# Chunks five to seven merged, v loaded an iteration sooner, range check in later pairs, units in two parts

## The chip, the cores and the metric

One core of one Trainium2 chip runs the whole program in one launch. The metric is device time in microseconds (us), the median of the runs shown. The core has TensorE (PE; the loading of its weights is shown as PEld), VectorE (DVE), ScalarE (ACT) and GpSimd (POOL), each with its own in-order queue, and SyncE (SP), whose queue issues nearly all DMAs.

## What is computed

A linear attention with decay (RWKV-5) feeds a feed-forward block with the SoLU activation. There are 4 batches, 8 heads, 768 steps and heads of 48.

```python
for t in range(S):
    kt, vt, rt = (k[:, :, t], v[:, :, t], r[:, :, t])
    cur = np.einsum('bhd,bhe->bhde', u[None] * kt, vt)
    y[:, :, t] = np.einsum('bhd,bhde->bhe', rt, state + cur)
    state = w[None, :, :, None] * state + np.einsum('bhd,bhe->bhde', kt, vt)
# x: y as (3072 tokens, 384)
h = x @ w_in                                  # 384 x 1024
sm = softmax(h);  solu = h * sm
ln = (solu - mean) / sqrt(var + 1e-6) * g_ln
out = ln @ w_out                              # 1024 x 384
```

All values are float32 except the two weight matrices, which the kernel is handed as 64-bit words and converts itself.

## The kernel before

The 768 steps of a batch are cut into six chunks of 128, so there are 24 units (chunk, batch), ordered chunk first: units 0 to 3 are the first chunk of each batch, 4 to 7 the second. "Chunk i" below is unit i. `direct_path` writes the order of the instructions on each engine out by hand; nothing reorders them.

**Stages of one chunk.** `load` (L464 on) asks for k and r into one of five `kpad`/`rpad` buffers and v into one of six `vt` buffers. POOL multiplies k by decay powers (`decay_k`, L701, gives `kp`) and r likewise for late chunks (`decay_r`, L708, gives `rp`), and forms r·u·k (`weigh`, L714 and L715); DVE sums that per head (`sum_own`, L719). `turn_r` and `turn_k` transpose on PE (L761, L769) with a DVE product (L762) and an ACT copy (L771) behind them. Chunks from `FIRST` = 9 on are transposed by DMA instead: `halve_k` (ACT, L1008) and `halve_r` (DVE, L1013) split 32-bit rows into 16-bit halves, SP issues the DMA transpose (L985), and `join_rk` (DVE, L990) puts the halves together.

The attention of a chunk comes in two forms, and `WHOLE` = 7 divides them. A **whole** chunk i < 7 takes its 128 steps at once: `whole_scores` (PE, L784), the diagonal by eight ACT operations (L729), `take_scores` (DVE, L810), then `whole_y` (PE, L841), which, from the second chunk of a batch on, first multiplies the carried state by r (the `state` rows of L841), and `whole_outer` (PE, L899) with `update` (DVE, L925 and L927) for the next state. A **merged** chunk i >= 7 takes two halves of 64 steps: `scores` (L802) and `outer` (L890) are called for two chunks by `attend`; the diagonal is two POOL selects (L734); `place` copies r's turned rows under the scores (ACT, L754 and L755, after a zero fill, L750, in its first four chunks); `middle` adds the first half's product to the state (DVE, L911); and `merged_y` (L863) needs no extra rows for the state, since state and r stand in the unused 48 of 64 rows of `vt` and of the score tile. POOL scales the state in `update` (L930). The rows of `vt` that stand unused are zeroed by twelve POOL memsets (L1132, L1133) just ahead of the loop.

The feed-forward part of a chunk: `take_y` (ACT, L874) moves y to `xT`; `ffn_in` (PE, L940) fills `h_ps`, of which there is one buffer, and ACT takes the exponential (L945); `unit` divides and multiplies on DVE (reciprocal L951, product L953), centres (ACT, L955) and squares (ACT, L962); `deviation` gives the reciprocal root on POOL, one column at a time (L967, L969); `halve_ln` (ACT, L996), a DMA transpose and `join_ln` (DVE, L990) give `lnT`; `ffn_out` (PE, L1035) multiplies by `w_out`, ACT scales (L1037), SP stores.

**Weights.** Fourteen pieces are converted: `convert_a` on ACT (L530), `convert_b` on DVE (L543, L545), `convert_c` on POOL (L553), and for pieces of `w_out` `convert_d` on DVE (L560). `take_up` is `convert_a` and the request for another piece. Later every piece is read again for a range check: `check_next` issues the load, and ACT (L571) and DVE (L573) reduce it; `check_sums` gathers the verdict near the end.

**Order.** A prelude handles chunks 0 to 2 with fillers on PE (`spin`). A loop over i = 2 to 6 takes one chunk per iteration: `ffn_in(i - 2)`, the turns of chunk i + 2, scores of i + 1, y of i. A first pair (i = 7), written out, and a loop of pairs (i = 9, 11, ...) follow; each pair has, on PE, `ffn_in(j)`, `attend`, `ffn_out(l)`, `ffn_in(j + 1)`, `ffn_out(l + 1)` and two `merged_y`, with j = i - 2 and l = i - 7.

## Time and profile before

| | |
|---|---|
| median of 3 runs | 335.6 us (335.38 to 340.46) |
| profiled execution as a whole | 337.11 us |
| its span, from first to last instruction | 335.3 us |
| PE busy | 323.0 us, 96% |
| DVE, ACT, POOL busy | 222.9, 231.1, 203.1 us |
| DMA | 52.59 MB, mean 157 GB/s |
| granted PE clock | 1.0 throughout |

In the profile, busy time counts instructions; the ends of matmuls are modelled, so neighbours on PE overlap by some tenths of a microsecond. "Idle before" is the time in which an engine stood still before an instruction, and the arrow names what ended it. The chain follows the last instruction back to what released it, step by step.

### The profile page before, as it was taken

The numbers are of one execution on the slowest core, as the hardware profiler recorded it, in microseconds if no ns is written. First come the engines' busy times: TensorE is split into PE (matmuls) and PEld (weight loads), VectorE is DVE, ScalarE is ACT, GpSimd is POOL, SyncE is SP. The second block draws the span as 40 slices with busy tenths as digits, with TensorE's granted clock in tenths as the row PEclk, the third lists the DMA queues.
The fourth block names the chain that finished last, engine by engine and source line by source line (L and its number), as shares of the span: only waits on it lengthen the run. The fifth ranks groups of instructions, "written<-read, shape, count | busy, mean of one in ns | idle before, by whom it ended". The sixth has DMA issues, their size and how long they took to land.

```text
span 335.3 us, 9036 instructions
## 1 busy us (share of the span) xinstructions
PE 323.0 (96%) x3667; PEld 192.3 (57%) x3667; DVE 222.9 (66%) x381; ACT 231.1 (69%) x393; POOL 203.1 (61%) x231
## 2 busy tenths in 40 slices
PE   8989899999999979999999999999999999999993
PEld 6956566665556546556556556556465555555572
DVE  8796889887964993995965975956927606333410
ACT  3776787986797776777677587588688386457411
POOL 6799988799999989679599389494150000000000
PEclk9999999999999999999999999999999999999999
DMA  7999999289799999999999998769485525355531
GB/s 149 235 269 220 206 238 158 34 143 167 159 197 191 170 214 188 144 185 168 189 201 142 148 217 148 155 168 208 71 153 126 118 72 133 65 133 134 134 90 31
DMA packets 165008, 52.59 MB, mean 157 GB/s; under 512 B 158173, under 2 KB 161374, under 8 KB 164958
## 3 DMA queue, kind: packets, MB, share of 16 engines
q1 hardware_dynamic: 164956, 51.92, 84.3%
q8 instruction: 31, 0.51, 0.7%
q14 instruction: 19, 0.16, 0.2%
q10 hardware_dynamic: 2, 0.00, 0.0%
HBM read 26.75 MB, written 4.72 MB: 94 GB/s over the span
## 4 chain that ended last, share of the span: by engine, by line
PE 68%; POOL 16%; DVE 5%; issue 4%; ACT 3%; DMA 2%; POOLq 0%; DVEq 0%; ACTq 0%
PE o_ps L1035 31%; PE h_ps L940 27%; POOL kp L701 4%; PE y_ps L863 4%; POOL rku L715 2%; POOL rku L714 2%; PE at L802 2%; POOL big L734 2%; DMA halves<-halves 2%; POOL rp L708 1%; PE kv_ps L890 1%; DVE ma L545 1%; POOL vt L1133 1%; PE y_ps L841 1%; POOL w_in_sb L553 1%
## 5 line engine op out<-in xcount | busy, mean ns | idle before, releaser
L940 PE MATMUL h_ps<-w_in_sb,xT 128*128 128x512 f32 x288 | 129.0, 597 | 2.4 <-ACT xT L874 2.4
L1035 PE MATMUL o_ps<-w_out_sb,lnT 128*128 128x384 f32 (+1 forms) x400 | 128.3, 476 | 0.0
L1035 PEld LDWEIGHTS o_ps<-w_out_sb,lnT 128*128 128x128 f32 x400 | 74.3, 190 | 48.6 <-issue 3.8
L940 PEld LDWEIGHTS h_ps<-w_in_sb,xT 128*128 128x128 f32 x288 | 53.5, 190 | 64.1 <-issue 57.0
L955 ACT ACTIVATE solu<-solu,st 128x1024 f32<-128x1024 f32 x24 | 27.5, 1148 | 36.2 <-DVE solu L953 36.2
L996 ACT COPY halves<-solu 128x2048 uint16<-128x2048 uint16 x24 | 45.3, 1889 | 1.1 <-DMA halves<-halves 1.0
L990 DVE COPY lnT<-halves 128x2048 uint16<-128x2048 uint16 x24 | 37.7, 1572 | 7.0 <-DMA halves<-halves 7.0
L930 POOL TENSOR_TENSOR vt<-vt,wide 48x384 f32<-48x384 f32 x16 | 19.6, 1238 | 31.9 <-DVE vt L927 31.6
L967 POOL TENSOR_SCALAR st<-st 128x1 f32<-128x1 f32 x24 | 6.7, 277 | 52.5 <-ACT e L962 52.3
L945 ACT ACTIVATE e<-h_ps 128x1024 f32<-128x1024 f32 x24 | 24.5, 1020 | 17.8 <-PE h_ps L940 17.8
L701 POOL TENSOR_TENSOR kp<-kpad,kdec 128x512 f32<-128x512 f32 x24 | 33.3, 1391 | 2.4 <-ACT kdec L652 1.6
L951 DVE RECIPROCAL st<-sums 128x1 f32<-128x1 f32 x24 | 3.8, 160 | 43.8 <-ACT e L945 43.7
L734 POOL TENSOR_SCALAR_AFFINE_SELECT big<-own 64x512 f32<-64x512 f32 x34 | 31.2, 919 | 2.2 <-PE y_ps L863 0.2
L953 DVE SCALAR_TENSOR_TENSOR solu<-h_ps,st,e 128x1024 f32<-128x1024 f32 x24 | 30.8, 1284 | 2.1
L1037 ACT ACTIVATE o<-o_ps,st 128x384 f32<-128x384 f32 (+1 forms) x25 | 14.0, 560 | 22.7 <-PE o_ps L1035 14.8
L714 POOL TENSOR_TENSOR rku<-kpad,u_bc 128x384 f32<-128x384 f32 x24 | 28.0, 1167 | 1.7 <-ACT u_bc L628 1.7
L715 POOL TENSOR_TENSOR rku<-rku,rpad 128x384 f32<-128x384 f32 x24 | 26.3, 1097 | 1.9
L573 DVE TENSOR_REDUCE least<-mag 128x1 f32<-128x384 f32 (+1 forms) x14 | 8.5, 607 | 26.6 <-ACT mag L571 26.6
L962 ACT ACTIVATE e<-solu 128x1024 f32<-128x1024 f32 x24 | 25.4, 1060 | 0.5
L815 DVE COPY_PREDICATED big<-later_half,at 64x512 f32<-64x512 uint32 x34 | 25.0, 734 | 0.4
L990 DVE COPY big<-halves 128x2048 uint16<-128x2048 uint16 x15 | 23.4, 1562 | 0.3
L708 POOL TENSOR_TENSOR rp<-rpad,rdec 128x512 f32<-128x512 f32 x15 | 22.3, 1486 | 0.0
(105 smaller groups left out, 406.1 us busy)
## 6 DMA issues: line engine op xcount, KB each, us to landing
raw<-in_moe_w_in_dram SPq DMA_DIRECT2D x12, 512.0 KB, 5.1
raw<-in_moe_w_out_dram SPq DMA_DIRECT2D x16, 384.0 KB, 4.0
kpad<-in_k_dram SPq DMA_DIRECT2D x24, 192.0 KB, 4.8
rpad<-in_r_dram SPq DMA_DIRECT2D x24, 192.0 KB, 5.2
out_dram<-o SPq DMA_DIRECT2D x23, 192.0 KB, 3.4
vt<-in_v_dram SPq DMA_DIRECT2D x34, 96.0 KB, 4.0
vt<-in_v_dram SPq DMA_DIRECT2D x7, 192.0 KB, 6.2
halves<-halves SPq DMA_TRANSPOSE x39, 5.0
```

The lines of the kernel that those rows point to most:

```text
L701: nc.gpsimd.tensor_mul(X["kp"].rearrange("p h d -> p (h d)"), kpads[i % NLD].rearrange("p h d -> p (h d)"), kdec.rearrange("p a d -> p (a ...
L708: nc.gpsimd.tensor_mul(X["rp"].rearrange("p h d -> p (h d)"), rpads[i % NLD].rearrange("p h d -> p (h d)"), rdec.rearrange("p a d -> p (a ...
L714: engine.tensor_mul(rku, kpads[i % NLD][:, :, 0:D], u_bc)
L715: engine.tensor_mul(rku, rku, rpads[i % NLD][:, :, 0:D])
L734: nc.gpsimd.affine_select(out=G[rows, c].rearrange("p a q u -> p (a q) u"), in_=X["own"][rows].to_broadcast([U, H, U]), compare_op=ALU.is_ ...
L940: nc.tensor.matmul(h_ps[:, ts(n, NX)], X["xT"][:, j, :], w_in_sb[:, j, ts(n, NX)], start=(j == 0), stop=(j == KD - 1))
L953: nc.vector.scalar_tensor_tensor(out=solu, in0=X["h"], scalar=rs, in1=X["e"], op0=ALU.mult, op1=ALU.mult, accum_out=tot)
L955: nc.scalar.activation(out=solu, in_=solu, func=ACT.Identity, scale=-float(dff), bias=tot)
L962: nc.scalar.activation(out=X["e"], in_=X["solu"], func=ACT.Square, accum_out=X["st"][0])
L990: nc.vector.tensor_copy(out=words.bitcast(U16).rearrange("p n (t o) -> p o n t", o=2), in_=turned)
L996: nc.scalar.copy(out=both.rearrange("p (o n) -> p o n", o=2), in_=split(X["solu"]))
L1035: nc.tensor.matmul(o_ps, X["lnT"][:, f, :], w_out_sb[:, f, part], start=(f == 0), stop=(f == KF - 1))
```

## The change

- `WHOLE` goes from 7 to 4: chunks 4, 5 and 6 (the fifth to seventh) take the merged form. The states in tiles of their own, the `state` rows of `whole_y` and the cases for them in `update` go. Chunk i + 1 is attended to in iteration i, and so is chunk 7 (in iteration 6 in place of the first pair); the order inside the loop is changed with it.
- The unused rows of `vt` are zeroed by six ACT fills in the prelude in place of the POOL memsets; the fills in `place` go.
- v is loaded one iteration sooner, for the merged chunks in two DMAs; the request for one weight piece moves behind.
- In the loop, `convert_c` stands after the turns, `take_up` ahead of the diagonal, and every other `convert_d` is on ACT.
- `unit` becomes `unit_a` (DVE) and `unit_b` (ACT); between the two stands `halve_ln`, which is thereby behind the exponential. `halve_rk` and `place` of the first two pairs move.
- `deviation` takes several columns at once from a common tile `stats`.
- `check_next` starts at pair i = 13, and is called twice a pair from i = 15.

```diff
-    LA, LO, FIRST, WHOLE = 2, 5, 9, 7
+    LA, LO, FIRST, WHOLE, CHECKED = 2, 5, 9, 4, 15
...
-    def convert_d(j):
+    def convert_d(j, scalar=False):
         dst, _, f = pieces[j]
         ma, low = step.pop(j)
         if f is not None:
-            nc.vector.tensor_scalar_mul(out=dst, in0=ma.bitcast(F32),
-                                        scalar1=minus_g[:, f : f + 1])
+            if scalar:
+                nc.scalar.activation(out=dst, in_=ma.bitcast(F32), func=ACT.Copy,
+                                     scale=minus_g[:, f : f + 1])
+            else:
+                nc.vector.tensor_scalar_mul(out=dst, in0=ma.bitcast(F32),
+                                            scalar1=minus_g[:, f : f + 1])
...
-    pairs = wpool.tile([128, 2, HP, 2, D], F32, tag="check", name="state", bufs=1)
-    third = wpool.tile([128, HP, 2, D], F32, tag="mag", name="state", bufs=1)
-    states = [pairs[:, 0], pairs[:, 1], third]
-    for St in states:
-        nc.scalar.activation(out=St.rearrange("p a q d -> p (a q d)"),
-                             in_=ident[:, 0:1].to_broadcast([128, dm]), func=ACT.Copy, scale=0.0)
...
+    for vt in vts:
+        nc.scalar.activation(out=vt[:, 1].rearrange("p h x -> p (h x)"),
+                             in_=ident[:, 0:1].to_broadcast([128, H * P]), func=ACT.Copy, scale=0.0)
...
+    stats = const.tile([128, 5, N], F32, name="stats")
...
-        if i < WHOLE + 4:
-            nc.scalar.activation(out=X["G"][32:64, 1].rearrange("p a q u -> p (a q u)"),
-                                 in_=ident[32:64, 0:1].to_broadcast([32, H * U]), func=ACT.Copy, scale=0.0)
...
-    def scores(chunks):
-        for n, i in enumerate(chunks):
+        for n, i in enumerate(chunks, at):
...
-        vt, AT, St = vts[i % NV], X["AT"], states[b] if c > 0 else None
+        vt, AT = vts[i % NV], X["AT"]
...
-        if c > 0:
-            for m in range(12):
-                a, n = divmod(m, 3)
-                into(m, St[:, a].rearrange("p q d -> p (q d)")[:, ts(n, 32)], X["rT"][:, a, :],
-                     False)
...
-            old = mid(i)[:, :, q] if i >= WHOLE else states[b][rows, :, q] if c > 0 else None
-            new = carried(i + B)[:, :, q] if i + B >= WHOLE else states[b][rows, :, q]
-            if old is None:
+            new = carried(i + B)[:, :, q]
+            if i < WHOLE:
                 nc.vector.tensor_mul(new, X["kv"][rows], wT)
             else:
-                nc.vector.tensor_add(new, X["kv"][1][rows] if i >= WHOLE else X["kv"][rows], old)
-        if i >= WHOLE or c > 0:
+                nc.vector.tensor_add(new, X["kv"][1][rows], mid(i)[:, :, q])
+        if i >= WHOLE:
             S = vts[(i + B) % NV][P : P + D, 0, :, 0:D]
             nc.gpsimd.tensor_mul(S, S, wide[P : P + D].unsqueeze(2).to_broadcast([D, H, D]))
...
-    def unit(i, later=False):
-        X = live[i]
-        st = small.tile([128, 8], F32, name="st", bufs=LO + 3)
-        rs, tot, ss, var, rstd = (st[:, n : n + 1] for n in range(5))
+    def unit_a(i):
+        X = live[i]
+        rs, tot, ss, var, rstd = (stats[:, n, i : i + 1] for n in range(5))
         nc.vector.reciprocal(out=rs, in_=sums[:, i : i + 1])
         solu = X["solu"] = fpool.tile([128, dff], F32, name="solu", bufs=LO)
         nc.vector.scalar_tensor_tensor(out=solu, in0=X["h"], scalar=rs, in1=X["e"],
                                        op0=ALU.mult, op1=ALU.mult, accum_out=tot)
+        X["st"], X["rstd"] = (ss, tot), rstd
+    def unit_b(i):
+        X = live[i]
+        solu, (ss, tot) = X["solu"], X["st"]
         nc.scalar.activation(out=solu, in_=solu, func=ACT.Identity, scale=-float(dff), bias=tot)
-        X["st"] = ss, var, rstd
-        if not later:
-            square(i)
-    def square(i):
-        X = live[i]
-        nc.scalar.activation(out=X["e"], in_=X["solu"], func=ACT.Square, accum_out=X["st"][0])
-    def deviation(i):
-        ss, var, rstd = live[i]["st"]
-        live[i]["rstd"] = rstd
+        nc.scalar.activation(out=X["e"], in_=solu, func=ACT.Square, accum_out=ss)
+    def unit(i):
+        unit_a(i)
+        unit_b(i)
+    def deviation(i, j):
+        ss, var, rstd = (stats[:, n, i:j] for n in (2, 3, 4))
         nc.gpsimd.tensor_scalar(out=var, in0=ss, scalar1=1.0 / dff, scalar2=1e-6 * dff ** 2,
                                 op0=ALU.mult, op1=ALU.add)
-        nc.gpsimd.tensor_tensor(out=rstd, in0=var, in1=neg_half, op=ALU.pow)
+        nc.gpsimd.tensor_tensor(out=rstd, in0=var, in1=neg_half.to_broadcast([128, j - i]), op=ALU.pow)
...
-    def take_up(p):
+    def take_up(p, more=1):
         nonlocal ahead
         convert_a(p)
-        if ahead < len(pieces):
-            load_weights(ahead)
-            ahead += 1
+        for _ in range(more):
+            if ahead < len(pieces):
+                load_weights(ahead)
+                ahead += 1
...
-    take_up(2)
+    take_up(2, 0)
...
     load(5, "kr")
     load(3, "v")
+    load(4, "v")
...
-    load(4, "v")
+    load(5, "v")
...
-    for vt in vts:
-        nc.gpsimd.memset(vt[:, 1, :, D:], 0.0)
-        nc.gpsimd.memset(vt[32:64, 1], 0.0)
     todo = list(range(6, len(pieces)))
     now = []
     for i in range(LA, LA + LO):
         j = i - LA
         load(i + 5, "kr")
-        load(i + 3, "v")
+        load(i + 4, "v")
         if i > LA:
             ffn_in(j)
         before, now = now, [todo.pop(0) for _ in range(2 if todo else 0)]
+        turn_r(i + 2)
+        turn_k(i + 2)
         for p in before:
             convert_c(p)
-        turn_r(i + 2)
-        turn_k(i + 2)
+        for p in now:
+            take_up(p)
         if i > LA:
             diagonal(i + 1)
             unit(j)
+        for p in before:
+            convert_d(p, p % 2)
         sum_own(i + 2)
         decay_k(i + 3)
         if i + 3 >= FIRST:
             decay_r(i + 3)
         weigh(i + 3, nc.gpsimd)
-        if 0 <= j - 1:
-            deviation(j - 1)
         if i - LO >= 0:
             halve_ln(i - LO)
         if i - LO - 1 >= 0:
             join_ln(i - LO - 1)
-        halve_rk(i + 3)
         if i + 1 < WHOLE:
             whole_scores(i + 1)
             take_scores(i + 1)
-        if i > LA:
+        else:
+            place(i + 1)
+            attend([i + 1])
+            middle(i + 1)
+        if LA < i < WHOLE:
             whole_y(i)
             take_y(i)
             whole_outer(i)
+        elif i >= WHOLE:
+            merged_y(i)
+            take_y(i)
+        if i > LA:
             update(i)
-        for p in now:
-            take_up(p)
-        if i == LA:
+        else:
             nc.vector.tensor_single_scalar(out=minus_g, in_=g_sb, scalar=-1.0, op=ALU.mult)
-        for p in before:
-            convert_d(p)
+        if i + 1 >= WHOLE:
+            take_scores(i + 1)
         for p in now:
             convert_b(p)
+        halve_rk(i + 3)
...
     diagonal(i + 1)
+    deviation(0, j)
     ffn_in(j)
     halve_k(i + 3)
-    attend([i, i + 1])
+    attend([i + 1], 1)
     unit(j)
     halve_r(i + 3)
-    place(i)
     place(i + 1)
     join_ln(l + 1)
     sum_own(i + 3)
-    take([i, i + 1])
-    load(i + 3, "v")
+    take([i + 1])
     load(i + 4, "v")
     diagonal(i + 2)
     decay(i + 4)
     diagonal(i + 3)
-    for n in (j - 2, j - 1):
-        if LO - 1 <= n:
-            deviation(n)
     decay(i + 5)
     halve_ln(l + 2)
     join_rk(i + 2)
-    check_next()
     ffn_out(l)
     load(i + 6, "kr")
     ffn_in(j + 1)
-    unit(j + 1, True)
-    halve_rk(i + 4)
+    unit_a(j + 1)
     load(i + 7, "kr")
     update(i)
     update(i + 1)
...
     for n in (i, i + 1):
         merged_y(n)
         take_y(n)
-    square(j + 1)
+    halve_rk(i + 4)
+    unit_b(j + 1)
     halve_ln(l + 3)
     join_ln(l + 2)
-    halve_rk(i + 5)
-    place(i + 2)
-    place(i + 3)
     sum_own(i + 5)
...
...
         for n in first + second:
             diagonal(n)
         decay(i + 4)
-        for n in (j - 2, j - 1):
-            if LO - 1 <= n < N:
-                deviation(n)
+        if j - 2 < N:
+            deviation(j - 2, min(j, N))
         decay(i + 5)
-        if l + 2 == N:
-            check_sums()
-        second_pair = i == LA + LO + 2
-        if l + 2 < N and not second_pair:
-            halve_ln(l + 2)
         if j < N:
             ffn_in(j)
         attend([i, i + 1])
         if j < N:
-            unit(j)
+            unit_a(j)
+        second_pair = i == LA + LO + 2
+        if second_pair:
+            place(i)
+            place(i + 1)
+        if l + 2 < N:
+            halve_ln(l + 2)
+        if j < N:
+            unit_b(j)
+        take([i, i + 1])
+        if second_pair:
+            halve_rk(i + 3)
         join_ln(l + 1)
         for n in first:
             join_rk(n)
-        take([i, i + 1])
-        if second_pair:
-            halve_ln(l + 2)
         if i + 4 < N:
             halve_rk(i + 4)
-        check_next()
+        if i >= CHECKED - 2:
+            check_next()
         ffn_out(l)
+        if l + 2 == N:
+            check_sums()
+        if j + 1 < N:
+            ffn_in(j + 1)
+            unit_a(j + 1)
         if l + 3 < N:
             halve_ln(l + 3)
-        if j + 1 < N:
-            ffn_in(j + 1)
-            unit(j + 1, True)
         for n in (i, i + 1):
             if n < N:
                 update(n)
...
                 merged_y(n)
                 take_y(n)
         if j + 1 < N:
-            square(j + 1)
+            unit_b(j + 1)
         if ahead_of_o:
             ffn_out(l + 1)
         halve_rk(i + 5)
...
             place(n)
         if l + 2 < N:
             join_ln(l + 2)
-        if i >= N - 7:
+        if i >= CHECKED:
             check_next()
```

More of the change, by code (lines that the diff above doesn't have):

```diff
@@ L786, in whole_scores, with scores @@
         X["scores"] = ps
-    def scores(chunks):
+    def scores(chunks, at=0):
         chunks = [i for i in chunks if i < N]
@@ L1038, in ffn_out, with attend, take @@
             nc.sync.dma_start(out=out[ds(b * S + c * T, T), part], in_=o[:, part])
+    def attend(chunks, at=0):
+        chunks = [i for i in chunks if i < N]
+        scores(chunks, at)
+        outer(chunks)
+    def take(chunks):
+        chunks = [i for i in chunks if i < N]
+        for i in chunks:
+            take_scores(i)
+        for i in chunks:
+            middle(i)
     ahead = 6
-    def take_up(p):
+    def take_up(p, more=1):
         nonlocal ahead
         convert_a(p)
-        if ahead < len(pieces):
-            load_weights(ahead)
-            ahead += 1
+        for _ in range(more):
+            if ahead < len(pieces):
+                load_weights(ahead)
+                ahead += 1
     turn_r(0)
@@ L1188, in check_next @@
             load_weights(p, "check", 1)
-    def attend(chunks):
-        chunks = [i for i in chunks if i < N]
-        scores(chunks)
-        outer(chunks)
-    def take(chunks):
-        chunks = [i for i in chunks if i < N]
-        for i in chunks:
-            take_scores(i)
-        for i in chunks:
-            middle(i)
     def decay(i):
```

## The prediction

> **What bounds the kernel now.** I read the page's engine shares and chain first, then the chain in order of time, then TensorE's own timeline around the changed chunks.
>
> ```profile
> PE 323.0 (96%) x3667; PEld 192.3 (57%) x3667; DVE 222.9 (66%) x381; ACT 231.1 (69%) x393; POOL 203.1 (61%) x231
> ...
> PE 68%; POOL 16%; DVE 5%; issue 4%; ACT 3%; DMA 2%; POOLq 0%; DVEq 0%; ACTq 0%
> ```
>
> TensorE (PE) is busy 96%, but it holds only 68% of the chain: for the other third some engine released it. The chain in order of time (start, us, what) shows where:
>
> ```profile
> 37.58 0.49 POOL vt L1133
> 38.15 1.27 POOL kp L701
> 39.47 0.66 PE tk_ps L769 x4
> ...
> 117.92 1.30 DVE solu L953 x2
> 119.27 1.03 issue
> 120.30 0.56 ACT o L1037
> 120.86 0.38 ACT xT L874
> 121.28 5.42 PE h_ps L940 x12
> ...
> 146.11 5.35 PE h_ps L940 x12
> ...
> 170.87 5.35 PE h_ps L940 x12
> ```
>
> From 121.28 to 329.62 every piece is PE: a pair of chunks each 146.11 - 121.28 = 24.8 us, no gap. Nothing that the change does for other engines after 121 us can shorten that. What can be won is the time at which this part begins. PE before it:
>
> ```profile
> 48.64 1.09 PE L784 MATMUL at<-big 48*64 48x128 f32 x32
> 49.66 0.86 PE L841 MATMUL y_ps<-big,state 128*32 128x128 f32 x24
> 50.34 1.06 PE L841 MATMUL y_ps<-big,vt 128*32 128x128 f32 x32
> 51.22 0.52 PE L899 MATMUL kv_ps<-vt,kp 128*32 128x48 f32 x32
> 51.67 5.42 PE L940 MATMUL h_ps<-w_in_sb,xT 128*128 128x512 f32 x12
> ...
> 74.54 1.16 PE L802 MATMUL at<-big 48*64 48x64 f32 x64
> 75.52 0.91 PE L890 MATMUL kv_ps<-vt,kp 64*48 64x48 f32 x64
> ...
> 92.03 2.00 PE L863 MATMUL y_ps<-big,vt 112*32 112x64 f32 x128
> 94.46 5.42 PE L940 MATMUL h_ps<-w_in_sb,xT 128*128 128x512 f32 x12 [0.43 <-ACT xT L874]
> ```
>
> Ends are modelled, so I price by starts. Idle PE between 20 and 122 us is 1.09 us (at 39.47, behind the POOL memsets L1132/L1133), 0.43 (94.46) and 2.00 (121.28): 3.5 us.
>
> **What the Trainium skill says.** "Perfetto Trace Analysis", Identifying the Most-Contended Engine: matmul busy share says little about the distance to the peak, since matmuls are pipelined. The trace agrees: the "96%" contains modelled overlaps; the gapless chain is the better evidence. "SBUF — State Buffer", Who interferes with whom: a VectorE instruction with two SBUF inputs and a GpSimd instruction that reads SBUF block each other. The trace fits: L545 takes 0.56 us or 1.07 to 1.28, the selects of L734 0.67 or about 0.97. So I give DVE and POOL work two prices. "ScalarE: Activation LUTs", What ACT_TABLE_LOAD costs: an activation is 186 ns + 0.833 ns per element, 93 more for a pointer operand, 93 overlapped in a row. The trace has 0.56 us for L1037 (384 elements, pointer scale). The page's table load of 1283 ns is the trace's 1.28 us.
>
> **The change, part by part.**
>
> *Merged chunks 4, 5, 6 (counted from 0), PE.* Per whole chunk with a state: scores 49.66 - 48.64 = 1.02, state rows 0.68, values 0.88, outer product about 0.35 (chain). Merged, per chunk: scores (75.52 - 74.54)/2 = 0.49 to 0.545 (chain: 1.09 for two), outer 0.36, y 1.93/2 = 0.97 (chain). In the loop's iterations i (32.52, 42.42, 51.67, 60.92 to 69.22 for 3 to 6): i=3 takes merged scores and outer of chunk 4 (0.9) for whole scores (1.02), -0.1. i=4 and i=5 lose 0.68 + 1.02 + 0.88 + 0.35 and get 0.9 + 0.97, -1.06 each. i=6 loses 0.68 + 0.88 + 0.35 and gets y 0.97 and the scores and outer of chunk 7 (0.9), about 0. The first pair has that 0.9 no more. PE work saved: 0.1 + 2.1 + 0.9 = 3.1 us, plus the 1.09 of idle time where the memsets stood: 4.2 us.
>
> *POOL.* Twelve memsets leave (32.9 to 38.15: 5.2 us). Six selects come (chunks 4 to 6, 0.67 to 0.97 each: 4.0 to 5.8) and 13 deviation pairs of 0.28 + 0.55..1.65 go by batching; the five-column power is not in the trace: from 0.55 (as one column) to five times that, I take 0.8. POOL then has in i=4 two L553 (2.0), two selects (1.6), kp 1.27, two rku (2.05), the state product 0.83: 7.8 us, under PE's 8.2. The stretch from 66 us to the second pair's last product loses about 2 us of deviations (0.74 + 1.93 + 1.5 go, some 1.1 + 0.8 come). Cover: POOL may run later than PE by what the prefetch of three chunks allows.
>
> *ACT.* Per chunk, eight diagonals (2.36 by starts) leave, four copies (L754/L755, 1.66) come. A scaled copy of a weight piece moves from DVE (0.39 to 0.95) to ACT (0.51 by the page, 0.56 by L1037). The four zero fills L750 (2.5) leave the first pairs. Six fills of 128x512 come early, between the u_bc copy (ends 5.5) and the kdec copy (9.23, after 3.71 us of idling): 6 x 0.52..0.63 = 3.1 to 3.8, so 0 to 0.1 us late; behind them wait kdec and POOL's kp: I take 0.1. The table load now stands behind u's DMA, which had landed by 3.39: 3.4 + 1.3 = 4.7, before u_ps is ready at 5.0. Nothing, and 1.3 us if that landing is later.
>
> *DVE.* Middle sums (two L911, 0.73) come, one scaled copy leaves: -0.2 to +0.4. The iteration 49.32 to 57.70 ran 8.38 us without a wait, so DVE stays at 8.2 to 8.6.
>
> *DMA and SP.* v is asked for an iteration earlier and in two DMAs; one weight piece is asked for later. v of chunk 4 left SP at 35.96 with kr of 6 and weight pieces 8 to 10 ahead of it; those now stand behind it, so it leaves near 31 and lands (6.2 us) by 38, when PE comes to it at 39. Price 0; up to 2 us if DMA, full until 58 us, delivers it later. Transposes keep their number.
>
> *Range checks later, units in two parts, splits behind exponentials.* Check pieces (0.87 ACT, 0.67 DVE, one DMA each) leave pairs one to three and make two per pair later, where ACT has 18 of 25 us and PE leads: 0. unit_a sets the division ahead of the joins and middle sums, so that the chain 109 to 121 (join, selection, middle, halves, check, division, ACT, xT) loses its last links: the 2.00 us go, and the 0.43. What is late next there: lnT of the second pair (transpose after the first pair's end), with about 1.5 us to spare by the same durations.
>
> *Sum.* The loop can't take all 3.3 us that PE saves up to 69.22. With 8.1 to 8.2 us of PE per iteration, the circle h (5.3), exponential (1.0), division (0.2 + 1.3) and handovers is 8.1 too (h_ps has one buffer), ACT in i=5 took 9.24 between exponentials (57.19 to 66.43) and now takes 9.24 - 2.36 + 1.66 + 0.5 = 9.0, and the next y waits for kT behind that exponential. So i = 3..6: 8.7, 8.4, 8.5, 9.0 = 34.6, from 32.6: h of chunk 5 begins at 67.2 (was 69.22), 2.0 ahead. First pair 0.9 less, with 0.3 lost as o_ps waits for a buffer that ACT frees: 2.6. Second: the idle 0.43 and 2.00: 5.0. The rest runs as before: 335.6 - 5.0 = 330.6. That profile's execution took 337.1 as a whole, span 335.3; the median of the runs is 335.6, and I subtract from that.
>
> **The rivals.** (a) *PE alone decides:* all 4.2 + 2.4 us come, 329.0. For it: PE held its pace until 57 us with DVE full. Against: ACT's 9.0 us in i=5. (b) *The gain is given back in the first pairs:* ACT and DVE keep 9 us in i=4..6, or joins wait for transposes (lnT waited 7.0 us in all); the lead stays at 2: 333.5. For it: that region was no PE region, from 60 to 119 us the chain runs through POOL, ACT, DVE and a transpose. Against: the work named has left just these queues. (c) *Slower:* rows are now split behind the exponential, near 8.4 us into the pair instead of at its start. The lnT join at the pair's end sits in DVE's order; when the transpose lands over 14 us later (measured: 5), the division and next h wait. Nine pairs at 1.4 us would cost 12.6 - 5.0: 343. Below that lateness it costs nothing. (d) *It doesn't do what it says:* the stages are all there in the built order; at most the zero fills could sit on the path, within 0.1.
>
> **How the numbers follow.** Likeliest case 0.55 at 330.6 (329.7 to 332), (a) 0.20 (328.3 to 329.6), (b) 0.19 (332 to 336), (c) and the like 0.06. The range reaches from (a)'s middle to (b)'s: 328.5 to 333.8, which has v's 2 us and the table load's 1.3 in it. Two per cent is 6.7 us, about what a measurement of this kernel can tell from no change: below 328.9 lies half of (a) and a little more, 0.14; above 342.3 0.06.
>
> **What would show it.** Right: no idle time before tk_ps of chunk 5; starts of h_ps about 8.5 us apart; h_ps of the third pair near 116; from there 24.8 us per pair. Wrong: h_ps waits for DVE's division or xT in later pairs; kv_ps waits for v; pairs of over 25 us; or no idle PE at all from 32 us on, which is (a).

## The result and the profile after

The changed kernel takes **333.81 us** (median of 4 runs, 333.49 to 333.98); before took 335.79 in the same measurement (4 runs, 335.38 to 340.46). The ratio is 0.994 [0.9925, 0.996]: 2.0 us faster, less than the 2% that count as a difference. Timed once more, it is 334.13 against 336.20, 0.993 [0.990, 0.996]. The forecast was 330.6 with a range to 333.8: a gain of 5.0 us, of which 2.0 came.

The page after, engine shares and chain by engine:

```profile
PE 321.1 (97%) x3691; PEld 190.1 (57%) x3691; DVE 222.9 (67%) x383; ACT 231.1 (70%) x384; POOL 188.4 (57%) x199
...
PE 83%; DVE 6%; ACT 3%; issue 2%; POOL 2%; DMA 2%; POOLq 0%
```

PE holds 83% of the chain instead of 68%; POOL fell from 16% to 2%. TensorE's timeline after (start, us, engine, line, operation, in brackets the idle time ahead of it and what ended it):

```profile
32.79 5.42 PE L932 MATMUL h_ps<-w_in_sb,xT 128*128 128x512 f32 x12
...
41.34 5.42 PE L932 MATMUL h_ps<-w_in_sb,xT 128*128 128x512 f32 x12
...
48.56 0.57 PE L883 MATMUL kv_ps<-vt,kp 64*48 64x48 f32 x30 [0.23 <-DVE big L760]
...
50.09 5.42 PE L932 MATMUL h_ps<-w_in_sb,xT 128*128 128x512 f32 x12
...
57.73 0.57 PE L883 MATMUL kv_ps<-vt,kp 64*48 64x48 f32 x30 [0.66 <-DVE big L760]
...
59.26 5.42 PE L932 MATMUL h_ps<-w_in_sb,xT 128*128 128x512 f32 x12
...
66.91 0.57 PE L883 MATMUL kv_ps<-vt,kp 64*48 64x48 f32 x30 [0.66 <-DVE big L760]
...
68.49 5.42 PE L932 MATMUL h_ps<-w_in_sb,xT 128*128 128x512 f32 x12
...
74.20 0.69 PE L800 MATMUL at<-big 48*64 48x64 f32 x32 [0.29 <-DVE big L813]
...
92.80 5.42 PE L932 MATMUL h_ps<-w_in_sb,xT 128*128 128x512 f32 x12
...
117.55 5.42 PE L932 MATMUL h_ps<-w_in_sb,xT 128*128 128x512 f32 x12
```

The reader is to see three things. The idle 1.09, 0.43 and 2.00 us of before are gone. Small new ones (0.23, 0.66, 0.66) stand in the loop, where PE waits for DVE's product L760, and one of 0.29 in the first pair, where it waits for DVE's selection L813. And chunk 5's `h_ps` starts at 68.49, only 0.73 us ahead of before, although the third pair's is 3.73 ahead. What DVE does in that loop, one iteration:

```profile
47.81 0.69 DVE L760 TENSOR_TENSOR big<-tr_ps,tab 128x512 f32<-128x512 f32 x1
48.42 0.15 DVE L942 RECIPROCAL stats<-sums 128x1 f32<-128x1 f32 x1
48.61 1.28 DVE L944 SCALAR_TENSOR_TENSOR solu<-h_ps,stats,e 128x1024 f32<-128x1024 f32 x1
49.82 0.08 DVE L944 DVE_READ_ACCUMULATOR solu<-h_ps,stats,e 128x1 f32 x1
49.82 0.65 DVE L564 TENSOR_SCALAR w_out_sb<-ma,minus_g 128x384 f32<-128x384 f32 x1
50.38 0.53 DVE L720 TENSOR_REDUCE own<-rku 128x8 f32<-128x384 f32 x1
50.93 0.72 DVE L904 TENSOR_TENSOR vt<-kv_ps,vt 48x192 f32<-48x192 f32 x2
51.68 0.72 DVE L919 TENSOR_TENSOR vt<-kv_ps,vt 48x192 f32<-48x192 f32 x2
52.44 1.52 DVE L813 COPY_PREDICATED big<-later_half,at 64x512 f32<-64x512 uint32 x2
53.99 0.79 DVE L543 TENSOR_SCALAR ma<-raw 128x384 uint32<-128x384 uint32 x1
54.81 0.56 DVE L545 SCALAR_TENSOR_TENSOR ma<-raw,ma 128x384 uint32<-128x384 uint32 x1
55.29 0.35 DVE L543 TENSOR_SCALAR ma<-raw 128x384 uint32<-128x384 uint32 x1
55.67 1.28 DVE L545 SCALAR_TENSOR_TENSOR ma<-raw,ma 128x384 uint32<-128x384 uint32 x1
56.99 0.69 DVE L760 TENSOR_TENSOR big<-tr_ps,tab 128x512 f32<-128x512 f32 x1
```

No wait stands in it, and it lasts 56.99 - 47.81 = 9.18 us. That is the interval at which `h_ps` comes (9.17, 9.23).

From `h_ps` of the third pair to the end the kernels agree: 335.3 - 121.28 = 214.0 us before, 331.8 - 117.55 = 214.25 after. The execution as a whole took 333.98 us, 2.2 outside the span, where before had 1.8.

### The profile page after: what moved, and what is told of

Same layout as the page of the kernel before. It is cut to its first block, busy times and chain, and to the rows that moved or that the text cites. A ratio compares the mean times of both kernels' runs of the same rounds, so it can differ in the third digit from the quotient of the medians.

```text
span 331.8 us, 9041 instructions
## 1 busy us (share of the span) xinstructions
PE 321.1 (97%) x3691; PEld 190.1 (57%) x3691; DVE 222.9 (67%) x383; ACT 231.1 (70%) x384; POOL 188.4 (57%) x199
## 4 chain that ended last, share of the span: by engine, by line
PE 83%; DVE 6%; ACT 3%; issue 2%; POOL 2%; DMA 2%; POOLq 0%
PE o_ps L1025 38%; PE h_ps L932 32%; PE y_ps L856 5%; PE at L800 3%; PE kv_ps L883 2%; DMA rpad<-in_r_dram 1%; DVE solu L944 1%; POOL kp L702 1%; DVE big L813 1%; DVE ma L545 1%; PE tk_ps L767 1%; POOL rku L716 1%; PE at L782 1%; DMA wq<-in_w_dram 1%; PE y_ps L839 1%
## 5 line engine op out<-in xcount | busy, mean ns | idle before, releaser
L922 POOL TENSOR_TENSOR vt<-vt,wide 48x384 f32<-48x384 f32 x16 | 19.6, 1241 | 38.8 <-DVE vt L919 38.4
L735 POOL TENSOR_SCALAR_AFFINE_SELECT big<-own 64x512 f32<-64x512 f32 x40 | 36.0, 899 | 2.4 <-PE y_ps L856 0.3
L1027 ACT ACTIVATE o<-o_ps,stats 128x384 f32<-128x384 f32 (+1 forms) x25 | 14.1, 564 | 32.5 <-PE o_ps L1025 20.3
L960 POOL TENSOR_SCALAR stats<-stats 128x2 f32<-128x2 f32 (+2 forms) x11 | 3.8, 343 | 54.7 <-ACT e L952 54.6
L702 POOL TENSOR_TENSOR kp<-kpad,kdec 128x512 f32<-128x512 f32 x24 | 31.5, 1315 | 3.8 <-ACT kdec L652 2.4
L944 DVE SCALAR_TENSOR_TENSOR solu<-h_ps,stats,e 128x1024 f32<-128x1024 f32 x24 | 30.8, 1284 | 2.2
L813 DVE COPY_PREDICATED big<-later_half,at 64x512 f32<-64x512 uint32 x40 | 29.6, 739 | 0.7
L951 ACT ACTIVATE solu<-solu,stats 128x1024 f32<-128x1024 f32 x24 | 27.6, 1149 | 2.6 <-DVE solu L944 2.6
L942 DVE RECIPROCAL stats<-sums 128x1 f32<-128x1 f32 x24 | 3.9, 161 | 35.4 <-ACT e L937 35.2
L715 POOL TENSOR_TENSOR rku<-kpad,u_bc 128x384 f32<-128x384 f32 x24 | 25.7, 1071 | 1.7 <-ACT u_bc L625 1.7
L856 PEld LDWEIGHTS y_ps<-big,vt 128*32 128x32 f32 (+1 forms) x1280 | 18.5, 110 | 5.3 <-issue 2.9
```

Source lines behind the costliest of these rows:

```text
L702: nc.gpsimd.tensor_mul(X["kp"].rearrange("p h d -> p (h d)"), kpads[i % NLD].rearrange("p h d -> p (h d)"), kdec.rearrange("p a d -> p (a ...
L715: engine.tensor_mul(rku, kpads[i % NLD][:, :, 0:D], u_bc)
L735: nc.gpsimd.affine_select(out=G[rows, c].rearrange("p a q u -> p (a q) u"), in_=X["own"][rows].to_broadcast([U, H, U]), compare_op=ALU.is_ ...
L813: nc.vector.copy_predicated(X["G"][rows, c].rearrange("p a q u -> p q a u"), later_half[rows].unsqueeze(1).to_broadcast([U, 2, HP, U]), X[ ...
L856: nc.tensor.matmul(y_ps[ts(g, 32), j, ts(c, U)], vf[:, at : at + 32], X["G"][rows, c, h // 2, h % 2, :], start=(g not in opened), stop=las ...
L944: nc.vector.scalar_tensor_tensor(out=solu, in0=X["h"], scalar=rs, in1=X["e"], op0=ALU.mult, op1=ALU.mult, accum_out=tot)
```

## The experiments

"Loop part" is the merging with all that goes with it up to the first pair (v, fills, copies); "pair part" is the range checks, the units in two parts, the splits. All start times are shifted by up to 1.0 us from execution to execution in the start-up, so the table gives `h_ps` of the third pair less `h_ps` of chunk 1.

| kernel | time against before | third pair less chunk 1, us | idle PE ahead of 2nd, 3rd pair |
|---|---|---|---|
| before (five profiles: 88.73 to 88.77) | 1 | 88.76 | 0.43, 2.00 |
| after | 0.994 [0.9925, 0.996] | 84.76 | 0, 0 |
| after again | 0.993 [0.990, 0.996] | 85.09 | 0, 0 |
| b_loop: loop part alone | 0.994 [0.991, 0.9965] | 85.40 | 0, 0 |
| b_pairs: pair part alone | 0.996 [0.994, 0.9975] | 86.21 | 0, 0 |
| b_fills | 0.998 [0.996, 1.001] | 88.36 | 0.42, 2.01 |
| b_no750 | 1.001 [0.999, 1.003] | 87.69 | 0, 1.25 |
| b_v | 1.003 [1.001, 1.005] | 88.75 | 0.43, 2.00 |
| b_v_no750 | 0.997 [0.996, 0.999] | 86.37 | 0, 0 |
| a_d_on_dve | 1.008 [1.005, 1.0115] | 89.51 | 0, 0 |
| a_no_545 | 0.993 [0.990, 0.996] | 84.94 | 0, 0 |
| a_c_later | 0.998 [0.996, 1.001] | 86.03 | 0, 0 |
| a_checks | 0.995 [0.993, 0.997] | 85.29 | 0, 0 |
| a_late_div | one execution, 333.96 us | 84.99 | 0, 0 |
| a_place | one execution, 335.31 us | 86.07 | 0, 0 |
| a_split | 0.993 [0.991, 0.996] | 85.07 | 0, 0 |

### What holds the loop

**a_d_on_dve**: DVE takes the scaled copies of both weight pieces, as before the change.

```diff
-            convert_d(p, p % 2)
+            convert_d(p)
```

> The changed kernel with every scaled copy of a weight piece on VectorE again, none on ScalarE. If VectorE bounds the loop of the changed kernel (9.2 us per iteration without a wait), an iteration grows by the copy's 0.56 to 0.78 us in i = 3 to 6: chunk 5's h_ps starts at 70.5 instead of 68.49 and the time is 335.6. If ScalarE bounds it (9.8 us between the exponentials around 60 us), or the landing of weight pieces does, the time stays at 333.8 or falls by up to 0.6.

The loop gets slower: chunk 5's `h_ps` starts at 71.60, with PE waiting for DVE (1.82 and 1.58 us ahead of `kv_ps`, 1.69 ahead of `at`), and the median is 4.6 us above that of after. DVE's iterations last 10.08 to 10.20 us, again without a wait, where those of after last 8.84 to 9.18. The two copies take 2.0 us together, where the one of after takes 0.65; they stand beside GpSimd's selects and L702. The granted clock was 0.83 from 50 to 60 us in this execution, but DVE had no wait in that stretch either, so the clock didn't set the pace. DVE is the bound, and one more copy costs it more than a copy's time alone.

**a_no_545**: the other direction, less work for DVE. The sign and top bit of `w_out` are not put back, so `w_out` is another matrix.

```diff
-        nc.vector.scalar_tensor_tensor(out=ma, in0=hi, scalar=0xC0000000, in1=part, ...
+        if pieces[j][2] is None:
+            nc.vector.scalar_tensor_tensor(out=ma, in0=hi, scalar=0xC0000000, in1=part, ...
```

> The kernel after, with the second DVE operation of a conversion (L545, 0.56 or 1.26 us) left out for the pieces of w_out: their sign and top exponent bit are not put back, so the output is not the reference's. All else stays in place. It takes 1.1 to 1.85 us from DVE in each of the loop's iterations that convert two such pieces. If DVE is what holds the iterations of chunks 3 to 5 at 9.2 us: h_ps starts come 8.4 to 8.6 us apart (PE and the circle of h, exponential and division are next), h_ps of chunk 5 starts near 67.0 instead of 68.5, the third pair's near 116.1, and the time is about 332.3. If ACT (9.8 us between two exponentials in one iteration) or the landing of weights and of kr holds them: the intervals stay above 9.0, h_ps of chunk 5 within 0.3 us of 68.5, and 333.8.

Intervals of 8.55, 8.34, 9.01 and 9.38 us: the iteration of chunk 3 gets 0.4 shorter, the two after it hardly change. ScalarE's timeline of this kernel shows the next bound for the last of them, an iteration without one wait from exponential to exponential:

```profile
55.82 1.02 ACT L938 ACTIVATE e<-h_ps 128x1024 f32<-128x1024 f32 x1
...
57.42 1.05 ACT L530 ACTIVATE low<-raw 128x384 uint32<-128x384 uint32 x2
58.60 1.15 ACT L952 ACTIVATE solu<-solu,stats 128x1024 f32<-128x1024 f32 x1
59.79 1.06 ACT L953 ACTIVATE e<-solu 128x1024 f32<-128x1024 f32 x1
...
60.84 0.60 ACT L562 ACTIVATE w_out_sb<-ma,minus_g 128x384 f32<-128x384 f32 x1
61.35 1.88 ACT L987 COPY halves<-solu 128x2048 uint16<-128x2048 uint16 x1
...
65.19 1.01 ACT L938 ACTIVATE e<-h_ps 128x1024 f32<-128x1024 f32 x1
```

That is 9.37 us. The iteration ahead of it takes ACT 9.03 us, of which 1.62 are a wait for a weight piece (L530 for the DMA into `raw`; after has the same 1.62): there a late weight piece is the next bound in this trace, more than ACT's own work. So DVE (9.2) holds chunks 3 to 5, and a late weight piece (9.0) and ACT (9.4) stand right behind it; both expectations were half right, and the median is 334.03, near after's 333.81 and 334.13.

**a_c_later**: a try to take the collision of L545 with GpSimd's L553 away.

```diff
+        if i > LA:
+            diagonal(i + 1)
         for p in before:
             convert_c(p)
...
-            diagonal(i + 1)
```

> The kernel after, with GpSimd's addition (L553) of both weight pieces put behind its selection of the diagonals, so that it doesn't run beside DVE's second L545. No work is left out. If the second L545 takes 1.26 instead of 0.56 us because L553 blocks it, and DVE holds the iterations: L545 is 0.56 both times, the interval falls from 9.2 to about 8.6, h_ps of chunk 5 starts near 67.2, time about 332.6. If the later addition delays the scaled copies of the weights, or the diagonals now run beside the conversion: L545 stays long or the scores wait for the diagonal, and 333.8 or up to 335.5.

It fails. The second L545 still takes 1.29 us, since the first L553 starts right after the first L545; the first now takes 0.88 in some iterations, and scaled copies up to 1.4. Chunk 5's `h_ps` comes 36.31 us after chunk 1's (35.70 in after). Which collisions occur depends on both queues, and moving one operation made others. PE also waited 1.65 us for the sums near the end of this execution.

### Which part takes the idle PE of the pairs

**b_pairs** is before with the pair part, **b_loop** before with the loop part. The pair part holds two more moves: `take`, the selections and middle sums, goes ahead of the joins on DVE, and the centring, now in `unit_b`, goes behind the copies to `xT` on ACT. The first line of each edit:

```diff
b_pairs
-    LA, LO, FIRST, WHOLE = 2, 5, 9, 7
+    LA, LO, FIRST, WHOLE, CHECKED = 2, 5, 9, 7, 15
b_loop
-    LA, LO, FIRST, WHOLE = 2, 5, 9, 7
+    LA, LO, FIRST, WHOLE = 2, 5, 9, 4
```

> The kernel before with the part of the change that lies in the pairs alone: units in two parts, splits of rows behind the exponential, range checks later, deviations for several columns; loop, chunks 4 to 6, loads of v and memsets as before. If the stalls of 0.43 and 2.00 us at the starts of the second and third pair were the ordinary state and go by this part, it takes 333.4 us. If ordinary executions have only about half of them (theory A), 334.3 us. If it only hides what TensorE covers anyway, 335.6.

> The kernel before with the loop part alone: chunks 4 to 6 merged, v an iteration sooner, fills on ACT, the copies and the scaled copies moved. The pair part (range checks later, units in two parts, splits behind exponentials) is left as before. The difference of after and the pair part alone says 0.4 to 0.7 us, ratio 0.998 to 0.999: h_ps of chunk 5 near 68.5, the idle stretches of 0.43 and 2.00 us come back ahead of h_ps of the second and third pair, third pair near 120.5. If the idle stretch at the third pair takes back what the loop gives (its chain goes through transposes and ACT, not through PE): it grows to 2.5 or more, third pair near 121.2, ratio 1.0. By my prediction's own sum for this part: chunk 5 at 67.2, third pair at 118.7 to 119, 333.0.

Each part alone takes away both idle stretches. Against before, b_loop gives 1.7 to 2.1 us and b_pairs 1.5, and both together 2.0 to 2.4: what the pair part adds to the loop part, some tenths of a microsecond, can't be told from nothing within these intervals. b_loop's TensorE timeline:

```profile
33.27 5.42 PE L931 MATMUL h_ps<-w_in_sb,xT 128*128 128x512 f32 x12
...
69.56 5.42 PE L931 MATMUL h_ps<-w_in_sb,xT 128*128 128x512 f32 x12
...
93.91 5.42 PE L931 MATMUL h_ps<-w_in_sb,xT 128*128 128x512 f32 x12
...
118.67 5.42 PE L931 MATMUL h_ps<-w_in_sb,xT 128*128 128x512 f32 x12
```

**a_late_div, a_checks, a_place** each move one step of the pair part in after. a_checks puts the range checks back into the early pairs. a_place puts the placements and splits back at the end of the first pair, and the second pair's split of rows behind the selections. a_late_div puts a pair's second division behind the state update; its expectation calls this the order of before, but before has that division ahead of `update` too, so it is later there than in either kernel.

```diff
a_late_div
             ffn_in(j + 1)
-            unit_a(j + 1)
...
                 update(n)
+        if j + 1 < N:
+            unit_a(j + 1)
a_checks
+    check_next()
     ffn_out(l)
...
-        if i >= CHECKED - 2:
-            check_next()
+        check_next()
...
a_place
+    halve_rk(i + 5)
+    place(i + 2)
+    place(i + 3)
     sum_own(i + 5)
...
-        if second_pair:
-            place(i)
-            place(i + 1)
-        if l + 2 < N:
+        if l + 2 < N and not second_pair:
             halve_ln(l + 2)
...
         if second_pair:
-            halve_rk(i + 3)
+            halve_ln(l + 2)
```

> The kernel after, with the first part of the second unit of a pair (the division on DVE) put behind the state update of the pair, as it stood before the change; the second part stays where it is. If the early division took the 2.00 us: 1 to 2 us of idle PE comes back ahead of h_ps of the third pair, waiting for ACT's xT or DVE's division, and the time is near 335. If other parts did (fills and placements out of ACT's way, joins by other order): the third pair starts at 117.6 as in after, 333.8.

> The kernel after, with the range checks of weights at their old places: one each in the first pairs, from the first pair on, and two in the last. All else as after. If the units in two parts and the splits behind exponentials took the two idle stretches of before (0.43 and 2.00 us ahead of h_ps of the second and third pair): no idle PE comes back, the third pair starts at 117.6, 333.8. If the shift of the checks took a part of them: 0.6 to 1.5 us of idle PE comes back ahead of h_ps of the second or third pair, 334.4 to 335.3. The time outside the span stays near 2.1 us if the checks have no part in it.

> The kernel after, with three steps put back where they stood in before: the placements of chunks 9 and 10 and the splits of chunk 12's r and k at the end of the first pair, and the second pair's split of rows behind the attention's selection. If these ACT steps ahead of the transposes took the 2.00 us: 1 to 2 us of idle PE come back ahead of h_ps of the third pair (near 118.6 to 119.6 instead of 117.6) and 334.8 to 335.8. If not: third pair at 117.6, 333.8.

The late checks are worth nothing here, and the second division may start 1.9 us later (114.24 against 112.33) at no cost. The placements and splits are worth something: 0.19 and 0.29 us of idle PE come back inside the second pair, and the third pair starts 1.0 to 1.3 us later than in after (86.07 against 84.76 to 85.09).

**b_fills, b_no750, b_v, b_v_no750** go into the loop part from the other side: before with the early fills of `vt` on ACT alone; without the fills L750; with v's loads an iteration sooner; with the last two together.

```diff
b_fills
+    for vt in vts:
+        nc.scalar.activation(out=vt[:, 1]..., func=ACT.Copy, scale=0.0)
...
-        nc.gpsimd.memset(vt[:, 1, :, D:], 0.0)
-        nc.gpsimd.memset(vt[32:64, 1], 0.0)
b_no750
-        if i < WHOLE + 4:
-            nc.scalar.activation(out=X["G"][32:64, 1]..., func=ACT.Copy, scale=0.0)
b_v
...
-        load(i + 3, "v")
+        load(i + 4, "v")
...
-    load(i + 3, "v")
```

> The kernel before with only the twelve GpSimd memsets of v's unused rows replaced by six ScalarE fills in the prelude. The idle 1.09 us of TensorE ahead of tk_ps of chunk 5 goes. If VectorE or ScalarE bounds iterations 4 to 6, chunk 5's h_ps starts less than 1.0 us earlier, and the stalls in the pairs give part of it back: 335.0 us. If TensorE bounds these iterations: 334.6, with h_ps of chunk 5 at 68.2 instead of 69.22.

> The kernel before with one thing less: the four zero fills on ACT (L750, 0.63 us each, two in the first pair's and two in the second pair's queue ahead of the exponential) are left out; they cover rows of the merged factors that meet zero rows of v, so all results are computed. Each of the two parts alone took away the idle 0.43 and 2.00 us. If ACT's queue ahead of the second pair's exponential (103.42 in before, 102.01 with the loop part alone, although that started 0.75 us later) is what makes the division and xT late: most of the 2.43 us go, the exponential comes at 102.2 or sooner, the third pair's h_ps starts 86.4 to 87.0 us after that of chunk 1 (88.76 in before, 85.40 with the loop part, 86.21 with the pair part), and the time is 0.994 to 0.996 of before. If it is the collision of the joins (2.38 and 2.12 us in before) with GpSimd, or the later transposes: 1.5 us or more of idle PE stay, 88.3 or more, and a ratio above 0.998.

> The kernel before, with v's loads alone moved an iteration sooner, as in the change; everything else, the zero fills too, as before. If SyncE's queue is what makes the joins and so the division and xT late: two requests for v instead of four stand ahead of the first pair's third transpose, the transposes leave 1.3 us or more sooner, and the third pair's h_ps starts 86.8 to 87.7 us after that of chunk 1 (88.76 in before), with 0.996 to 0.999 of the time. If those requests cost nothing, as I predicted: 88.3 or more, idle 0.43 and 2.00 us again, ratio 1.0.

> The kernel before, with v's loads an iteration sooner and without the four zero fills on ACT (L750; all results are computed). If v's requests and the fills together are what the loop part removes in the pairs: no idle PE ahead of h_ps of the second and third pair, the third pair 86.2 to 86.5 us after chunk 1 (before 88.76 less 2.43), ratio 0.994 to 0.997. If something else in the loop part is needed: 0.7 us or more of idle PE stay.

b_fills: the 1.09 us behind the memsets go, and a wait of 0.87 us for DVE's division takes their place; 0.4 us are left of it. b_v changes nothing in the trace, as I had priced it (its median lies 0.3% above before's), although the two requests fewer (2.69 to 1.31 us of SyncE's queue) are plainly there: the transpose behind them leaves no sooner (88.56 us, against 88.38 in before). Without the fills 1.2 of 2.43 us go in the trace and nothing in the median; with v's loads as well, all of the 2.43 go, and the median falls by 0.8 us. So v's loads help only beside the other step. But then b_v_no750's timeline goes on like this:

```profile
119.66 5.42 PE L937 MATMUL h_ps<-w_in_sb,xT 128*128 128x512 f32 x12
...
133.99 5.39 PE L937 MATMUL h_ps<-w_in_sb,xT 128*128 128x512 f32 x12 [1.75 <-DVE solu L950]
...
146.85 5.42 PE L937 MATMUL h_ps<-w_in_sb,xT 128*128 128x512 f32 x12 [0.38 <-ACT xT L871]
```

The idle time moved one pair on. The chain of that stretch runs through `DMA halves<-halves` (two transposes, 12.27 us): ACT's split L993 waits 1.75 us for them and starts at 129.34, the exponential stands behind it (131.14), and DVE's division waits for the exponential. In before the exponential came at much the same time (130.30) and PE, later by itself, hid it. In after the exponential stands ahead of that split (124.64).

### Where the rest of the lead goes

**b_again, b_p1, b_p2, b_p3** are before unchanged, profiled again; **a_again** is after unchanged; **a_split** is after with the last sums' DVE operations ahead of the last join.

```diff
a_split
+        if l + 2 == N:
+            low = check_sums()
         join_ln(l + 1)
...
-            check_sums()
+            check_flag(low)
```

> The kernel before, unchanged, profiled a second time. The first profile of it belongs to an execution of 337.1 us, 1.5 us above the median of 335.6. Theory A (the first profile held idle time of TensorE that most executions don't have): this profile has a span near 333.8 us and less than the 3.5 us of idle TensorE between 20 and 122 us of the first one, above all less than the 2.00 us at the third pair's start. Theory B (the two kernels differ in what lies outside the span): a span of 335.3 us again, with the same 2.00 us.

> The kernel before, unchanged, profiled once more. If the idle stretches differ from execution to execution: among this and the next two, one at least has under 1.5 us of idle PE ahead of the second and third pair's h_ps, and a span of 334.5 or less. If they are in every execution: 2.3 to 2.5 us each time, and the span goes by start-up, clock and tail alone.

> The kernel before, unchanged. As for the run before it: under 1.5 us of idle PE in one of the three, or 2.3 to 2.5 us in each.

> The kernel before, unchanged. As for the two runs before it: under 1.5 us of idle PE in one of the three, or 2.3 to 2.5 us in each.

> The kernel after, unchanged, timed against before on the same chip. If the gain in time is what the first measurement said: ratio 0.993 to 0.996, some 1.5 to 2.3 us, 2.0 to 2.2 us outside the span. If the executions of before that were timed first were short ones: the ratio is 0.990 to 0.993.

> The kernel after, with the seven DVE operations of the final check of sums put ahead of the last join of rows; its matmul stays between the last two output products. No work is left out. In after the check's reduction ended 0.25 us before PE came to its matmul, and in two other kernels PE waited there, 1.25 and 1.65 us, because the last transpose landed later. If that wait strikes executions of after too: no wait of n_ps for DVE, a smaller scatter, and 333.2 to 333.6 in the median. If it doesn't: 333.8, the same as after. If the 0.3 to 0.5 us more outside the span come from the check's later place: the time outside the span falls from 2.1 towards 1.8 us.

All profiled executions of before have the 0.42 to 0.45 and 1.98 to 2.01 us. They took 337.1, 338.1, 338.7, 339.1 and 337.4 us, every one above the median, 336.4, of the 100 executions of before that were timed beside the first sixteen runs. Two of them, p1 and p2, also had a dip of the granted clock after 125 us (215.5 and 215.9 us from the third pair's start to the end, where the others have 213.7 to 214.3). After's two profiled executions (333.98, 334.13) lie at its medians. So the traces of before overstate the ordinary execution by 1 us or more, and after's don't. The clock isn't the reason: of the 140 executions of before that were timed beside all the runs, the 32 with a granted clock of 0.999 or 1.0 have a median span of 334.2 us, and the two traced ones at that clock have 335.3 and 335.5. The excess lies inside the span. b_v_no750 says the same more strongly: its profile with the 2.13 us of moved idle took 337.64, its median is 335.15. That ordinary executions have shorter idle stretches is the reading that fits; no trace of one shows it, so it is argued, not shown. b_loop, without these stretches, was traced 0.9 us above its median too, with 0.64 us of waiting for the sums near its end. One rival is untested: in each of its seven measurements the execution of before that is listed first, though not traced, lies above the median (336.65 to 340.46), so a first execution may be longer for another reason.

a_split's scatter (333.4 to 335.4) is no smaller than that of after again, its ratio is the same, and the time outside the span stays at 2.1. The wait for the sums is real in single executions, as in this line of a_no_545, but the median of after doesn't hang on it:

```profile
321.69 0.19 PE L688 MATMUL n_ps<-ones,low 128*1 128x1 f32 x2 [1.25 <-DVE low L686]
```

## Why the prediction was wrong

**Held.** No idle PE ahead of `tk_ps` of chunk 5. PE with one gap of 0.29 us from the first pair on, then 24.75 us a pair. The early ACT fills and v's loads cost nothing that shows beside the shift of the start-up. The second and third pair lose the 0.43 and 2.00 us. The third pair's `h_ps` was to start near 116; it starts at 117.55.

**The step that failed: "DVE stays at 8.2 to 8.6".** The intervals were put at 8.7, 8.4, 8.5, 9.0 and were 8.55, 8.75, 9.17, 9.23. Against the iteration of before that I built on (8.38 us), the middle sums came as priced (+0.75). The half-height select takes 0.16 more (1.52 against 1.36), which I had left out. The scaled copy that stays takes 0.65, where the two of before took 0.77, so 0.12 leaves and not 0.4 to 0.95. One L543, beside GpSimd's state product (L922), takes 0.79 instead of 0.34. Only an L545 of 0.56 in place of 1.07 helps. Together some +0.7 to 0.8: 9.1 to 9.2. There was a slip too: 8.38 with -0.2 to +0.4 is 8.2 to 8.8, not 8.6. The two prices for DVE's work beside GpSimd were in the text, but the iteration that I built on held both copies in 0.77, and the work that stays meets other neighbours in its new place. ACT's "9.0" is 9.37 (in a_no_545). At chunk 5 the lead is 0.73 instead of 2.0 us, and 0.27 of the missing 1.27 are a later start of chunk 1's `h_ps` (32.79 against 32.52); the same 1.27 is missing at the third pair, 5.0 - 3.73. It is rival (b)'s first clause, "ACT and DVE keep 9 us in i=4..6". The time is (b)'s too, but by luck: the lead was not given back in the first pairs and didn't stay at 2, it grew there to 3.73, and the rest went as the next paragraph says.

**The second: the subtraction from the median.** I took 3.73-odd us seen in a trace of 337.1 us from a median of 335.6. The sum in measured terms: 3.73 lead at the third pair, less 0.23 in the stretch after it and 0.37 outside the span, is 3.13, which is 337.11 - 333.98. Of that, 1.32 is the profiled execution's distance from before's median of 335.79, and 0.17 after's own: 3.13 - 1.32 + 0.17 = 1.98. I had named that distance and still counted the 2.43 us of idle in full. b_no750 took 1.07 us off the path in its trace and nothing off the median.

**Right by size, wrong by cause.** I credited the 2.43 us to the division's earlier place, "ahead of the joins and middle sums". The code doesn't do that: a pair's first division stood there already, and the second stands behind them in both kernels. What moved are the selections and middle sums, and the centring. The second pair before, DVE and ACT:

```profile
107.33 2.38 DVE L990 COPY lnT<-halves 128x2048 uint16<-128x2048 uint16 x1 [1.09 <-DMA halves<-halves]
109.61 2.12 DVE L990 COPY big<-halves 128x2048 uint16<-128x2048 uint16 x1
111.62 2.97 DVE L815 COPY_PREDICATED big<-later_half,at 64x512 f32<-64x512 uint32 x4
...
117.92 1.28 DVE L953 SCALAR_TENSOR_TENSOR solu<-h_ps,st,e 128x1024 f32<-128x1024 f32 x1
...
119.25 1.15 ACT L955 ACTIVATE solu<-solu,st 128x1024 f32<-128x1024 f32 x1 [3.95 <-DVE solu L953]
...
120.76 0.85 ACT L874 COPY xT<-y_ps 128x384 f32<-128x384 f32 x2
```

And after:

```profile
101.64 2.98 DVE L813 COPY_PREDICATED big<-later_half,at 64x512 f32<-64x512 uint32 x4
...
107.30 2.12 DVE L980 COPY lnT<-halves 128x2048 uint16<-128x2048 uint16 x1
109.32 2.12 DVE L980 COPY big<-halves 128x2048 uint16<-128x2048 uint16 x1
...
112.33 1.28 DVE L944 SCALAR_TENSOR_TENSOR solu<-h_ps,stats,e 128x1024 f32<-128x1024 f32 x1
...
117.69 0.48 ACT L867 COPY xT<-y_ps 128x384 f32<-128x384 f32 x1 [0.42 <-PE y_ps L856]
118.07 1.15 ACT L951 ACTIVATE solu<-solu,stats 128x1024 f32<-128x1024 f32 x1
```

DVE selects while the transpose is on its way, and the copies to `xT` no longer stand behind a centring that waits for the division. a_late_div leaves both moves in place; no run takes back either alone, so which of them the pair part's gain hangs on is not shown. What is shown: the loop part alone takes both stretches away without these moves, and v's loads with the fills gone do it in the trace. What I had priced as two gains of separate origin was one, reached from two sides.

**Open.** Why the pair part adds 0.3 to 0.5 us outside the span (means of the timed executions: 1.78 before, 1.75 with the loop part alone, 2.27 with the pair part alone, 2.07 to 2.10 after). The later place of the sums' reduction on DVE isn't it (a_split), nor the range checks (a_checks, 2.08).

## What to carry to other kernels

When an engine is relieved at a saturated stage, add up each other engine's iteration with every operation at the price that it has beside its neighbours, and take the longest: here PE can do an iteration in 8.3 us (a_no_545), DVE took 9.2 and ACT 9.4, and relieving PE only laid bare the other two. An idle stretch in a trace counts as a gain only if what is late next (here the next pair's transposes) isn't late by the same amount. It may also be longer in the traced execution than in ordinary ones: profile the kernel before more than once and compare with the median before subtracting. Two edits that remove the same wait are worth it once.

## What was not expected of the hardware

- DVE's L545 (two inputs from SBUF) takes 0.56 us alone and 1.26 to 1.29 while GpSimd's L553 runs, which keeps its own 1.0. In the iteration of after shown above, L553 starts at 55.54, L545 at 55.67, and L545 ends 0.4 us after L553 does, so it stood still for most of it. The Trainium skill, "SBUF — State Buffer", Who interferes with whom, calls the pair of ports that the two engines share an exclusive lock and says that the order of issue decides who blocks; the trace agrees.
- The last transpose of rows landed 5.4 us after its split in after, and 7.0 in a_no_545, the same code at that place; that made the 1.25 us of idle PE near the end.
